# Attention into SwiGLU on one core: the transposes of half-batch 4 moved from TensorE to DMA

## The chip, the cores and the metric

The kernel runs on one core of a Trainium2 chip. The metric is the device time of one execution in microseconds (us), taken as the median of several runs. A profile is one further execution with its own time.

A core has five engines, each with its own queue of instructions that it works through in order: TensorE (PE, with PEld for its weight loads), VectorE (DVE), ScalarE (ACT), GpSimd (POOL) and SyncE (SP). In this kernel SyncE does no arithmetic: it issues transfers. Results of matmuls lie in eight PSUM banks, which other engines read and so free again.

## The reference

For 8 batches of 8 heads, 576 positions and 64 dimensions, causal attention with a decay term taken from `s`, and then a SwiGLU block over all 4608 tokens with `DM` = 512 and `DF` = 1536:

```python
scores = scale * np.matmul(q, k.transpose(0, 1, 3, 2))
cum = np.cumsum(np.maximum(s, 0.0), axis=-1)
bias = -(cum[:, :, :, None] - cum[:, :, None, :])
scores = np.where(causal, -1000000000.0, scores + np.minimum(bias, 0.0))
attn = np.exp(scores - np.max(scores, axis=-1, keepdims=True))
attn = attn / (np.sum(attn, axis=-1, keepdims=True) + 1e-09)
x = np.matmul(attn, v)          # to (B*S, H*D)
g = x @ w_gate
out = (g * (1.0 / (1.0 + np.exp(-g))) * (x @ w_val)) @ w_out
```

## The kernel before

Heads are numbered 0 to 63 (`bh`, or `kk` in the loop). Four heads make a half-batch (`hb`, 0 to 15), eight a batch. For each half-batch, k and q arrive as float32 (`load_qk`, L140, tiles `rawk` and `rawq` with three buffers), are cast to bfloat16 (`cast_one`, L244 on ScalarE or L246 on the others, tiles `ck` and `cq`) and have to be transposed into the score operand `KQ[hb % 2]`, of which there are two. Its other rows, `aug`, carry the decay term and come by DMA from `HL` (L183).

There are two ways to transpose. Half-batches below `NPE` = 5 go over TensorE: `prep_one` transposes 128x128 blocks with the identity (L287), five or four to a bank, and `pe_out` copies each bank out in two halves (L314 on ScalarE, L316 on VectorE). Half-batches from 5 on go over a scratch in DRAM: `scratch` writes `ck` and `cq` to `ks` and `qs` (L260), `transposes` reads them back with two transposing DMAs into `pk` and `pq` (L270), all issued by SyncE, and `split` copies the halves into `KQ` on VectorE (L274, four copies per half-batch). `pk` and `pq` have one buffer each.

For each head, `score_piece` makes four chunks of scores (L359), ScalarE takes the exponential into `pt` (L369), GpSimd masks the diagonal chunks (L374, L379), `av_piece` multiplies by V (L396), and VectorE divides by the row sum (`rc` L412, `ot` L413). V arrives in five chunks per batch (`load_v`, L157, one buffer `rawv`) and is cast into `VT` (L166, L168). The result, transposed into `XT`, feeds the second block: in tiles of 512 tokens, gate and value products (L629), a tanh on ScalarE (`th`, L650), two VectorE instructions that free the gate bank and the value bank (`pp` L652, `ht` L663), and the output product (L686, or L735 in a form with seven products).

The order of all instructions is written by hand (`manual_schedule`). After a prologue with heads 0 to 7, the loop at L1003 walks through the items of the nine token tiles and, between them, pumps `attn_items`, which walks through heads 8 to 63. Loads, casts, scratch writes, transposes and copies of coming half-batches are hung onto certain heads (`h`, `step`) and chunks (`ci`) in `side`. Copies of `split` go onto a list, `later`, from which the loop takes one at some items, and all at the first head of a half-batch. SyncE's queue keeps the program's order: an issue that waits for a cast or for another transfer holds every issue behind it.

The part that matters lies around heads 12 to 20 (`h` = 3 and 4). In the kernel before, SyncE there has, in this order: five loads of V 1, loads of k and q 4, of k and q 5 (all in the prologue), five loads of V 2 (issued at head 12), k and q 6, the scratch writes and transposes of half-batch 5 (head 16), k and q 7, two chunks of V 3, the scratch writes of half-batch 6, three chunks of V 3, the transposes of half-batch 6. Here V n is batch n's V.

Of the kernel before, what the change touches and what calls it, by code (L numbers as in the profile page):

```python
# [19 lines left out]
def kernel(  # L20
# [14 lines left out]
    B, H, S, D = q.shape  # L35
# [6 lines left out]
    NHB = BH // HB  # L42
    NR = HB // 2
# [33 lines left out]
        tc.tile_pool(name="dram", bufs=1, space=bass.MemoryType.DRAM)  # L77
    )

    NPE = 5  # L80
    XB = 2
    KS = {i: dram.tile([NR * S, 128], BF16, name=f"ks{i}") for i in range(NPE, NHB)}
    XS = {
        i: dram.tile([NCH * 128, 128], BF16, name=f"xs{i}") for i in range(XB * H // 2, BH // 2)
    }
    QS = {i: dram.tile([NR * S, 128], BF16, name=f"qs{i}") for i in range(NPE, NHB)}

# [16 lines left out]
    first = first_sbuf.enter_context(tc.tile_pool(name="first", bufs=1))  # L104
# [5 lines left out]
    with tc.manual_schedule():  # L110
# [36 lines left out]
        def load_qk(hb):  # L147
            load_one(hb, "k")
            load_one(hb, "q")

        def load_v(b, cs, eng=nc.sync):
            if 0 in cs:
                loaded["v", b] = raw.tile([128, NCH, H, D], FP32, tag="rawv", bufs=1, name="rawv")
            t = loaded["v", b]
            for c in cs:
                n = 128 if c < 4 else TAIL
                eng.dma_start(  # L157
                    t[0:n, c, :, :],
                    v[b, :, c * 128 : c * 128 + n, :].rearrange("h p d -> p h d"),
                )  # L160
# [97 lines left out]
        def scratch(hb):  # L258
            for name, SC in (("k", KS), ("q", QS)):
                nc.sync.dma_start(  # L260
                    SC[hb].rearrange("(x j) c -> x (j c)", j=J),
                    cts[name, hb].rearrange("x j r d -> x (j r d)"),
                )
# [3 lines left out]
        def transposes(hb):  # L267
            for name, SC in (("k", KS), ("q", QS)):
                prs[name, hb] = cp.tile([128, NR * S], BF16, tag="p" + name, bufs=1, name="p" + name)
                nc.sync.dma_start_transpose(prs[name, hb], SC[hb])  # L270
# [184 lines left out]
        later = []  # L455

        def do_later(n):
            while n > 0 and later:
                f, *args = later.pop(0)
                f(*args)  # L460
                n -= 1
# [5 lines left out]
        def side(h, step, ci):  # L467
            bh = HB * h + step
            for c in V1_AT.get((bh, ci), ()):
                cast_v(1, c, nc.gpsimd)  # L470
            if bh == H + 4 and ci == 3:
                load_v(2, range(5))
            if h == 4 and (step, ci) in ((0, 1), (2, 1)):
                load_qk(6 + step // 2)
            if h >= 5 and h + 3 < NHB and (step, ci) == (0, 1):
                load_qk(h + 3)
            hb = h + 1
            if NPE <= hb < NHB:
                late = hb == NPE
                if late and (step, ci) == (0, 1):  # L480
                    scratch(hb)
                if late and (step, ci) == (0, 3):
                    transposes(hb)
                if (step, ci) == (0, 1):
                    aug(hb, GP4)
                first = 1 if hb < NPE + 3 else 0
                if step in (first, first + 1) and ci == (3 if late else 1):
                    for r in range(NR):
                        later.append((split, hb, "kq"[step - first], r))
            hb = h + 2  # L490
            if hb == NPE and step == 3 and ci % 2 == 1:
                cast_one(hb, "kq"[ci // 2], nc.gpsimd)
            if NPE < hb < NHB:
                six = hb == NPE + 1
                if (step, ci) == ((2, 0) if six else (0, 2)):
                    cast_one(hb, "k", nc.scalar)
                if (step, ci) == ((2, 2) if six else (1, 2)):
                    cast_one(hb, "q", nc.scalar)
                if (step, ci) == ((3, 0) if six else (2, 0)):
                    scratch(hb)  # L500
                if (step, ci) == (3, 3 if six else 0):
                    do_later(NR * 2)
                    transposes(hb)
            if ci != 1:
                return
            bn = h // 2 + 1
            if 3 <= bn < B:
                if h % 2 == 0:
                    if step == 2:
                        load_v(bn, (0, 1))  # L510
                    if step == 3:
                        load_v(bn, (2, 3, 4))
# [4 lines left out]
        def side_v(h, step, ci):  # L517
            bn = h // 2 + 1
            if h == 4 and (step, ci) in V2_AT:
                cast_v(2, V2_AT[step, ci], nc.gpsimd)  # L520
            if 3 <= bn < B and h % 2 == 1 and (step, ci) in V_AT:
                cast_v(bn, V_AT[step, ci], nc.scalar)
# [3 lines left out]
        def prep_one(hb, i, eng=None):  # L526
# [7 lines left out]

        PREP_AT = {
            2: {(1, 2): 0, (2, 0): 2, (2, 2): 1, (3, 0): 3},
            3: {(1, 3): 0, (2, 1): 1, (2, 3): 2, (3, 1): 3},
        }

        AV_AT = {  # L540
# [6 lines left out]
        def attn_items():  # L547
            for kk in range(H, BH + 2):
                h, step = divmod(kk, HB)
                if kk < BH:  # L550
                    if step == 0:
                        do_later(NR * 2)
                    if step == 1 and 3 < h + 1 < NPE:
                        cast_one(h + 1, "k", nc.gpsimd)
                        cast_one(h + 1, "q", nc.gpsimd)
                    if step == 2 and 3 < h + 1 < NPE:
                        aug(h + 1, GP4)
                    for ci in range(4):
                        score_piece(kk, ci)
                        side(h, step, ci)  # L560
                        side_v(h, step, ci)
                        yield kk + 0.1 + ci / 8
                        if (step, ci) in PREP_AT.get(h, ()):
                            prep_one(
                                h + 1, PREP_AT[h][step, ci],
                                (nc.scalar, nc.vector)[ci // 2] if h == 2 else None,
                            )
                            yield kk + 0.1 + ci / 8
                for x in X_AT.get(kk, (kk - 2,)):
                    if x % 2 == 1 and H <= x < BH:  # L570
                        if x < XB * H:
                            x_pe(x // 2)
                            yield kk + 0.5
                        else:
                            x_in(x // 2)
                for p in AV_AT.get(kk, (kk - 1,)):
                    if H <= p < BH:
                        av_piece(p, (0, 1, 2))
                        yield kk + 0.6
                        av_piece(p, (3,))  # L580
                        yield kk + 0.7
                        av_piece(p, (4,))
                        av_out(p)
                        if p >= XB * H and p % 2 == 1:
                            x_out(p // 2)
                        yield kk + 0.8
# [369 lines left out]
        aug(3, SP4)  # L956
        load_v(1, range(5))
        load_qk(4)
        load_qk(5)
        x_pe(0, nc.vector)  # L960
        values(4, 5)
        x_pe(1, nc.scalar)
# [40 lines left out]
        for tt in range(NTT):  # L1003
            lo = H * (tt + 1) + LAGS[tt]
            hi = min(H * (tt + 2) + LAGS[tt + 1], BH + 2)
            span = 36 if tt < FIRST7 else 34.5
            if hi == BH + 2:
                span = 30
            n0 = 5 if tt == 0 else 0
            n = 0  # L1010
            todo = {FIRST7 - 1: W_SUMS, FIRST7: W_DIFFS}.get(tt, [])
            if tt == FIRST7:
                for _ in range(3):
                    weight_op(*todo.pop(0))
            for i, cost in enumerate(ffn_items(tt)):
                n += cost
                if todo and (i >= 24 if tt < FIRST7 else i % 2 == 1):
                    weight_op(*todo.pop(0))
                if tt == 0 and n > 30:
                    pass  # L1020
                elif i >= 2 * NFT or i % (2 if tt == 1 else 4) == 1:
                    do_later(1)
                if seconds:
                    seconds.pop(0)()
                for f in hook.pop(n, ()):
                    f()
                done = min(1.0, max(0, n - n0) / (span - n0))
                if tt == 0:
                    done = (
                        0.57 * max(0, n - n0) / (24 - n0) if n < 24  # L1030
                        else min(1.0, 0.57 + 0.43 * (n - 24) / (span - 24))
                    )
                pump(lo + (hi - lo) * done)
# [31 lines left out]
```

## Time and profile before

| | |
|---|---|
| median of 3 runs | 377.03 us (375.74 to 377.14) |
| the profiled execution's own time | 375.79 us |
| its span (first to last instruction) | 374.0 us |
| granted TensorE clock | 0.999 |
| TensorE busy | 360.7 us, 96% |
| VectorE, ScalarE, GpSimd busy | 289.6, 240.4, 212.3 us |
| hardware DMA queue (SyncE's) | 41.46 MB, 45.2% of 16 engines' span |
| software DMA queue (GpSimd's) | 22.21 MB, 22.6% |

The page cuts the span into 40 slices of 9.35 us, with a digit per slice for the busy tenths of each engine. The chain of waits goes back from the last instruction to whatever released it, step by step. The order in time lists the instructions of one engine with start, duration, line, output and input; in brackets stands how long the engine stood idle before and what ended that. "SPq" rows are SyncE's issues, not the transfers: their duration is the time for which SyncE was held by the issue. The trace also has a record of each semaphore that a transfer fills when it has landed; these are the landing records.

### The profile page before, as it was taken

Reading aid. Unit: us, or ns where it says so; the run is one execution under the profiler, and the core shown is the slowest. Engines: PE = TensorE matmul, PEld = TensorE weight load, DVE = VectorE, ACT = ScalarE, POOL = GpSimd, SP = SyncE. Lnnn points to the kernel's source line nnn. Section 1 sums busy time; section 2 is a strip of 40 time slices with the busy share of each in tenths; the row PEclk is TensorE's granted clock in tenths of the full one; section 3 lists DMA queues with packets and bytes.
Section 4 is the critical chain, followed back from the end, with each engine's and each line's share of the span. In section 5 each row is a group of like instructions: output and inputs, shape, how many; then the busy total and the mean of one; then the engine's idle time right before and its main releaser. Section 6 shows DMA issues by size and latency. Waiting matters only on the chain.

```text
span 374.0 us, 8759 instructions
## 1 busy us (share of the span) xinstructions
PE 360.7 (96%) x3259; PEld 230.6 (62%) x3300; DVE 289.6 (77%) x578; ACT 240.4 (64%) x471; POOL 212.3 (57%) x325
## 2 busy tenths in 40 slices
PE   7799899999999999999999999999999999999995
PEld 6584456655555556855685559655865585476464
DVE  8968776468995899588967997699858867975984
ACT  8777677698876877588757875686566523323321
POOL 8883555856455647494649464955675516315320
PEclk9999999999999999999999999999999999999999
DMA  7899999799877997896779675984132103002003
GB/s 239 193 258 253 219 257 267 237 303 247 245 186 220 254 262 196 178 281 205 211 167 266 178 182 174 255 206 98 40 119 62 35 19 128 2 0 95 20 0 114
DMA packets 97146, 64.23 MB, mean 172 GB/s; under 512 B 77232, under 2 KB 82736, under 8 KB 97104
## 3 DMA queue, kind: packets, MB, share of 16 engines
q1 hardware_dynamic: 84976, 41.46, 45.2%
q0 software_dynamic: 12128, 22.21, 22.6%
q8 instruction: 26, 0.43, 0.5%
q14 instruction: 16, 0.13, 0.1%
HBM read 37.90 MB, written 19.86 MB: 154 GB/s over the span
## 4 chain that ended last, share of the span: by engine, by line
PE 85%; DMA 6%; POOL 5%; ACT 1%; issue 1%; DVE 1%; DVEq 0%; POOLq 0%; ACTq 0%
PE bank L629 45%; PE bank L735 17%; PE bank L359 10%; PE bank L396 7%; PE bank L686 5%; DMA rawk<-in_k_dram 4%; DMA rawv<-in_v_dram 2%; POOL rawv L157 1%; POOL vt L168 1%; POOL wv L332 1%; ACT pt L369 1%; PE bank L287 0%; POOL rawq L140 0%; ACT kq L314 0%; POOL kq L211 0%
## 5 line engine op out<-in xcount | busy, mean ns | idle before, releaser
L369 ACT ACTIVATE pt<-bank 128x512 bf16<-128x512 f32 (+1 forms) x256 | 120.4, 510 | 31.0 <-PE bank L359 18.2
L629 PE MATMUL bank<-XT,wg 128*128 128x512 bf16 x418 | 110.3, 379 | 1.2 <-DVE pp L652 0.3
L629 PE MATMUL bank<-XT,wv 128*128 128x512 bf16 x412 | 109.3, 379 | 1.1
L650 ACT ACTIVATE th<-bank 128x512 bf16<-128x512 f32 x108 | 64.7, 599 | 55.9 <-PE bank L629 53.6
L652 DVE SCALAR_TENSOR_TENSOR pp<-th,bank 128x512 bf16<-128x512 bf16 x108 | 73.6, 682 | 19.2 <-ACT th L650 18.7
L663 DVE SCALAR_TENSOR_TENSOR ht<-pp,bank 128x512 bf16<-128x512 bf16 x108 | 74.1, 686 | 10.6 <-PE bank L629 0.4
L359 PE MATMUL bank<-kq 128*128 128x128 bf16 (+4 forms) x576 | 75.6, 240 | 1.5 <-DMA kq<-HL 1.0
L672 POOL TENSOR_TENSOR ht<-ht 128x512 bf16<-128x512 bf16 x35 | 40.4, 1154 | 52.2 <-DVE su L670 52.1
L359 PEld LDWEIGHTS <-kq 128*128 128x128 bf16 x576 | 45.8, 98 | 31.5 <-issue 1.9
L629 PEld LDWEIGHTS <-wv 128*128 128x128 bf16 x432 | 38.4, 98 | 36.5 <-issue 0.6
L629 PEld LDWEIGHTS <-wg 128*128 128x128 bf16 x432 | 38.3, 98 | 34.2 <-issue 0.7
L396 PEld LDWEIGHTS <-pt 128*128 128x128 bf16 x960 | 41.9, 98 | 17.2
L374 POOL TENSOR_SCALAR_AFFINE_SELECT pt<-pt 128x512 bf16<-128x512 bf16 x56 | 36.8, 658 | 27.3 <-ACT pt L369 22.7
L396 PE MATMUL bank<-vt,pt 128*128 128x65 bf16 x960 | 47.0, 194 | 0.4 <-POOL vt L168 0.3
L430 POOL DMA_DIRECT2D xs<-ot x24 | 21.7, 905 | 30.0 <-DVE ot L413 27.6
L735 PEld LDWEIGHTS <-ht 128*128 128x128 bf16 x336 | 31.2, 98 | 4.3
L413 DVE TENSOR_TENSOR ot<-bank,rc 128x320 bf16<-128x320 f32 x64 | 31.5, 492 | 2.2
L183 POOL DMA_DIRECT2D kq<-HL x48 | 28.9, 604 | 0.0
L735 PEld LDWEIGHTS <-su 128*128 128x128 bf16 x252 | 23.5, 98 | 3.3
L686 PE MATMUL bank<-wo,ht 128*128 128x512 bf16 x90 | 24.8, 379 | 0.3
L800 POOL TENSOR_TENSOR ysb<-ysb 128x512 f32<-128x512 f32 x12 | 15.2, 1270 | 15.3 <-DVE ysb L794 15.3
L379 POOL TENSOR_SCALAR_AFFINE_SELECT pt<-pt 128x64 bf16<-128x64 bf16 x56 | 14.8, 264 | 15.8 <-ACT pt L369 15.7
(93 smaller groups left out, 384.6 us busy)
## 6 DMA issues: line engine op xcount, KB each, us to landing
out_dram<-ysb POOLq DMA_DIRECT2D x32, 256.0 KB, 4.5
rawv<-in_v_dram SPq DMA_DIRECT2D x28, 256.0 KB
rawk<-in_k_dram SPq DMA_DIRECT2D x12, 576.0 KB
rawq<-in_q_dram SPq DMA_DIRECT2D x12, 576.0 KB
xs<-ot POOLq DMA_DIRECT2D x24, 160.0 KB, 3.5
ks<-ck SPq DMA_DIRECT2D x11, 288.0 KB
qs<-cq SPq DMA_DIRECT2D x11, 288.0 KB
rawk<-in_k_dram POOLq DMA_DIRECT2D x3, 576.0 KB, 7.3
```

The source lines that it names most:

```text
L359: nc.tensor.matmul(sc[:, o : o + w], T[:, 1, e * S + 128 * tj : e * S + 128 * (tj + 1)], T[:, 0, e * S + lo : e * S + hi], start=not maske ...
L369: nc.scalar.activation(pt[:, c0 : c0 + n], sc, AF.Exp, scale=0.125)
L374: nc.gpsimd.affine_select(pt[:, 1088:1600], pt[:, 1088:1600], pattern=[[0, 4], [1, 128]], compare_op=ALU.is_ge, fill=zreg, base=0, channel ...
L396: nc.tensor.matmul(av[:, bi * (D + 1) : (bi + 1) * (D + 1)], pt[:, c0 : c0 + 128], VT[b % 2][:, tj, h, :], start=(tj == 0), stop=(tj == bi),)
L413: nc.vector.tensor_mul(ot[:, :, e * D : (e + 1) * D], av3[:, :, 0:D], rc[:, :, None].to_broadcast([128, NCH, D]),)
L629: nc.tensor.matmul(view(bs, TT), w[:, c, f0 : f0 + 128], xt[:, c, :], start=(c == 0), stop=(c == 3),)
L650: nc.scalar.activation(th, pg, AF.Tanh, scale=0.5)
L652: nc.vector.scalar_tensor_tensor(pp, in0=th, scalar=1.0, in1=pg, op0=ALU.add, op1=ALU.mult)
L663: nc.vector.scalar_tensor_tensor(hp[:, 2 * k2 : 2 * k2 + 2, :].rearrange("p a n -> p (a n)"), in0=pp, scalar=0.5, in1=pv, op0=ALU.mult, op ...
L672: (nc.vector if ft == NFT - 1 else nc.gpsimd).tensor_sub(hp[:, 1:3, :], hp[:, 1:4:2, :], hp[:, 0:3:2, :])
L686: nc.tensor.matmul(view(pys[ts_], DM), hps[ft // 2][:, 2 * (ft % 2) + half, c0 : c0 + 128], WO[j][:, ft % WKO, :], start=(ft == 0), stop=( ...
L735: nc.tensor.matmul(ps, lhs(p), rhs(p), start=(first and p == 0), stop=(last and p == NP - 1), skip_group_check=True,)
```

## The change

`NPE` becomes 4, so half-batch 4 no longer goes over TensorE, and gets scratch tensors `ks4` and `qs4`. A new constant `NSC` = 5 keeps the places of all later half-batches as they were. For half-batch 4 the scratch writes are issued at head 13, chunk 3, and its transposes at head 14, chunk 0; the loads of k and q 5 move from the prologue to directly behind these, and the five loads of V 2 from head 12 to behind those. Its four copies are put on `later` at heads 14 and 15, and the loop now takes them in the stretch of the first token tile where it took nothing. The casts of half-batch 4 stay on GpSimd at head 13.

By engine: TensorE loses 18 transposes, ScalarE four copies out of PSUM; on VectorE four copies out of PSUM make way for four out of `pk` and `pq` at nearly the same places, and the rest of its order is unchanged; GpSimd's order is unchanged; SyncE gets two scratch writes and two transposes between the loads of q 4 and k 5, and the rest of its order is unchanged.

```diff
-    NPE = 5
+    NPE = 4
+    NSC = 5
@@ side(h, step, ci)
-            if bh == H + 4 and ci == 3:
-                load_v(2, range(5))
+            if h == 3:
+                if (step, ci) == (1, 3):
+                    scratch(4)
+                if (step, ci) == (2, 0):
+                    transposes(4)
+                    load_qk(5)
+                    load_v(2, range(5))
+                if (step, ci) in ((2, 3), (3, 1)):
+                    for r in range(NR):
+                        later.append((split, 4, "kq"[step - 2], r))
@@ (further down in side: every NPE becomes NSC)
-            if NPE <= hb < NHB:
-                late = hb == NPE
+            if NSC <= hb < NHB:
+                late = hb == NSC
...
@@
         PREP_AT = {
             2: {(1, 2): 0, (2, 0): 2, (2, 2): 1, (3, 0): 3},
-            3: {(1, 3): 0, (2, 1): 1, (2, 3): 2, (3, 1): 3},
         }
@@ attn_items
-                    if step == 1 and 3 < h + 1 < NPE:
+                    if step == 1 and h == 3:
                         cast_one(h + 1, "k", nc.gpsimd)
                         cast_one(h + 1, "q", nc.gpsimd)
-                    if step == 2 and 3 < h + 1 < NPE:
+                    if step == 2 and h == 3:
                         aug(h + 1, GP4)
@@ prologue
         load_qk(4)
-        load_qk(5)
@@ main loop
                 if tt == 0 and n > 30:
-                    pass
+                    if later and later[0][1] == 4:
+                        do_later(1)
```

## The prediction

> **What bounds the kernel now.** I read the page first (span, engines, the 40 slices), then the table of busy time by stages, then the chain of waits around the change (50 to 90 us), then the order in time of SyncE's issues, POOL and DVE there. Half-batch n holds heads 4n to 4n+3; "k 4", "V 2" and so on name a transfer's data.
>
> ```profile
> span 374.0 us, 8759 instructions
> PE 360.7 (96%) x3259; PEld 230.6 (62%) x3300; DVE 289.6 (77%) x578; ACT 240.4 (64%) x471; POOL 212.3 (57%) x325
> PEclk9999999999999999999999999999999999999999
> DMA  7899999799877997896779675984132103002003
> ```
>
> TensorE is busy 96% of the span and its clock is never lowered, so what comes off PE's queue is time won, and an interval in which PE must stand is time lost. DMA is near nine tenths through the first quarter: a transfer put into that stretch delays the transfers behind it. By stages:
>
> ```profile
> 60.00:70.00 10.00, 9.89 (x130) 6.79 (x130) 6.91 (x15) 5.90 (x12) 5.00 (x8) 1.00 0.95 255
> 70.00:80.00 10.00, 9.89 (x86) 5.71 (x87) 2.85 (x7) 8.97 (x18) 9.51 (x18) 1.00 0.79 208
> 80.00:90.00 10.00, 9.77 (x101) 5.75 (x101) 8.72 (x18) 7.62 (x15) 5.12 (x10) 1.00 1.25 321
> ```
>
> (Columns: stretch, length, then busy us of PE, PEld, DVE, ACT, POOL, clock, DMA share, GB/s.) The removed work lies in the first of these, where PE is full and DVE and ACT are not. In the last, DVE is close to full: it could not catch up there. SyncE's issues:
>
> ```profile
> 54.18 9.56 SPq L157 DMA_DIRECT2D rawv<-in_v_dram  x5
> 63.85 0.55 SPq L140 DMA_DIRECT2D rawk<-in_k_dram  x1
> 68.21 0.36 SPq L260 DMA_DIRECT2D ks<-ck  x1
> 69.49 0.35 SPq L260 DMA_DIRECT2D qs<-cq  x1
> 71.14 1.74 SPq L270 DMA_TRANSPOSE pk<-ks  x1
> 72.98 1.29 SPq L270 DMA_TRANSPOSE pq<-qs  x1
> ```
>
> Five V issues take 9.56 us although one alone takes 0.37 to 0.6: SyncE is held by its own full queue. The trace's landing records (when a transfer's semaphore is full) show the queue served in order: q 4 at 56.5, q 5 59.8, V 2 61.0 to 66.3, k 6 67.9, q 6 69.4, ks 5 70.2, qs 5 71.4, pk 5 75.3, pq 5 77.3, q 7 81.9, pk 6 93.1. On the other side stand those who use them:
>
> ```profile
> 56.88 1.15 POOL L246 CAST cq<-rawq 128x1152 bf16<-128x1152 f32 x1 [1.45 <-DMA rawq<-in_q_dram]
> 79.58 0.45 DVE L274 COPY kq<-pk 64x1152 bf16<-64x1152 bf16 x1
> 79.95 0.67 DVE L652 SCALAR_TENSOR_TENSOR pp<-th,bank 128x512 bf16<-128x512 bf16 x1
> 84.39 0.95 DVE L274 COPY kq<-pq 64x1152 bf16<-64x1152 bf16 x1
> ```
>
> and, in the chain of waits, PE's first score of half-batch 5 (head 20):
>
> ```profile
> 85.37 0.12 issue
> 85.49 0.38 PE bank L359 x4
> ```
>
> The copy out of pk 5 starts 4.3 us after pk 5 has landed, and head 20's score starts 0.15 us after the first copy out of pq 5 (84.39 + 0.95 = 85.34): that score has no slack against DVE.
>
> **The change, part by part** (times on the clock of this profile).
>
> *Removed from PE, ACT, DVE.* 18 transposes (L287); between other matmuls the chain of waits books five at 0.28 us and four at 0.22, together 1.0 us, from a PE that is full: −1.0. Bounds: 0, if a later wait takes it, and −2.2, with the 1.2 us for which DVE stood waiting for these L287 added. ACT loses four copies (1.5 + 1.5 us), DVE four (1.6 + 1.4), and gains four copies out of pk and pq at 0.45 = 1.8 us: nothing, since both have 3 us free in 10 there. Four banks fewer are taken: nothing.
>
> *Half-batch 4 by DMA.* The casts stay where they are on POOL: ck 4 ends 54.30 + 1.13 = 55.4, cq 4, which waits for q 4, ends 58.0. SyncE issues ks 4 at 55.5 and qs 4 at 58.1 (0.36). pk 4 is issued at 58.5 (ks landed 2.0 us after its issue for half-batch 5, so by 57.5), and pq 4 when qs has landed, about 60.1, until 61.4. A transpose landed 4.2 and 4.3 us after its issue: 62.7 and 64.4. The four copies stand on DVE where the four L316 stood (61.9 to 68.3): the first comes about 62.8 and the third, out of pq 4, about 65.8; head 16's score comes at 67.9 (68.90 less 1.0). Cost 0, with some 0 to 3.5 us of cover; 2 us at most if the transposes take half as long again.
>
> *What stands behind them on SyncE.* k 5 and q 5 are now issued at 61.4 instead of 45.6, V 2 after that, then k 6 and q 6, ks 5, qs 5 and pk 5. q 7 landed 4.6 us after pq 5, so q 5 lands at 64.4 + 4.6 = 69.0, 9.2 us later than now. V 2 needs 6.5 us (59.8 to 66.3): 75.5. k 6 77.1, q 6 78.6, ks 5 79.4. pk 5 is issued then and lands 4.2 later: 83.6, against 75.3 now, +8.3; pq 5 about 85.5. Bounds: without the stores to out that shared the DMA while q 7 came, q 5 lands 3.1 us after pq 4 (as q 6 after V 2), and T4 might take 1 us less: +5.5; with these stores (73 to 80 us) now beside V 2 and half-batch 6: +10.5. I keep 8.3.
>
> *Waiters in between.* POOL's cq 5 cast (68.32) waits for q 5 till 69.0; behind it on POOL stand a mask (L374, 70.03) and four aug issues, all with about 2 us before use: 0, at most 1. ACT's cast of k 6 (76.51, 75.5 after the gain) waits till 77.1 with th (L650) and exps behind it: up to 1.6, which eats the 1.0 won but falls ahead of the next, longer wait, so it isn't added. V 2's casts on POOL (74.38 to 79.1) come after their landing (70.2 to 75.5): 0.
>
> *DVE at pk 5, the step that decides.* DVE reaches the first copy of half-batch 5 at about 79.6 (78.6 if the whole gain got there) and stands till 83.6. Behind it wait pp (79.95), which frees a gate bank, ht, rc and ot. PE takes that gate bank again at 81.70, so it runs on for 2.1 us and then stands. From 83.6 DVE works through its 4.8 us of queue up to the copy out of pq 5, which ends 0.45 to 0.95 later: 83.6 + 4.8 + 0.6 = 89.0. Head 20's score starts at 89.1 in place of 85.49: **+3.6** net, the 1.0 already inside. Bounds by pk 5's: +0.8 (80.8) to +5.8 (85.8).
>
> *Half-batch 6.* It has less slack: pk 6 landed at 93.1 and its copy started at 93.77, that is 97.4 in the shifted time; behind pq 5 the queue is full up to there (q 7, V 3, ks, qs), so pk 6 keeps about 8 of its 8.3 us: 101. DVE stands 3.5 us, PE is covered for about 2.1 to 2.5: **+1.0** (0 to +3.5). Head 24's score (103.01 + 3.6 = 106.6) then finds its copies done at 101 + 5.3 = 106.3. At half-batch 7 the copy (109.14) came 3.4 us after pk 7 (105.7), and SyncE stood 3 us for ks 7, so with 4.6 us of compute shift the queue has caught up: 0.
>
> Sum: +4.6 against the profiled execution's 375.8: 380.4. The median of the runs is 1.2 above that execution, which makes 381.6; I take 381.0, between.
>
> *A rule weighed.* Rows: nine blocks by DMA landed in 4.2 us, about 0.47 us each, and PE did one in 0.056 us of its queue. The Trainium skill (VectorE: DVE Perf Modes, "The three transpose paths" and the rules below it) says to use TensorE for 128×128 where PSUM will do and gives 1309 ns for the DMA way. An estimate by that figure, 18 × 1.3 = 23.6 us in a row, would land pq 4 near 82, put head 16 some 14 us late and the time near 390. The row is a third of it, so it decides; the rule's direction stands against this change.
>
> **Rivals.**
> - *The queue catches up* (the other side). The hardware queue fills 45% of the engines over the span, and V 2 no longer has k 5, q 5 and the weights' tail ahead of it. If pk 5 lands by 79.6, head 20 is not late; at 78.6 or before, the whole 1.0 stays: 376.0 on the runs' scale, at best 374.8 with the 1.2 above. That needs a shift of pk 5 below 3.3 us where the two transposes alone hold the queue from 58.5 to 64.4. Against it: the order of landings.
> - *The delay stays*: half-batches 6 and 7 wait too, PE's cover being used up by a DVE that is 87 to 90% busy. PE then ends with all of pk's 8.3: 377.0 + 8.3 = 385.3.
> - *Half-batch 4 itself is late*: pq 4 after 67.9 rather than 64.4 (q 4 later, or transposes at half speed) moves head 16 and everything behind; 2 us more: 383.5.
>
> **How the numbers follow.** Half a per cent is 1.9 us, about what a measurement of this kernel tells from no change. Forecast (+2.5 to +6.5) 0.56; delay stays 0.13; half-batch 4 late 0.09; queue catches up or lands near 80 us (−2.2 to +1.9) 0.22, of which over 1.9 us faster 0.05. So faster 0.05, same 0.17, slower 0.78. The range, 376.0 to 386.0, takes in the rival at its working value and the whole 8.3; the forecast's own is 379 to 384.
>
> **What will show it.** Right: SyncE's k 5 issue near 61 to 62 and pk 5 near 79; a DVE idle of 3 to 5 us before L274, released by DMA pk; head 20's L359 about 3.6 us later; L287 18 fewer. Wrong: no DVE idle before L274 between 75 and 100 us (then the queue was not full), or the first idle already at head 16.

## The result and the profile after

The changed kernel takes 382.07 us (median of 5 runs, 380.71 to 384.54) against 377.03 before. The ratio on record, taken from the runs of the two, is 1.0159 with a 95% interval of 1.0122 to 1.0196; the two medians alone give 1.0134. The profiled execution took 384.54 us, the slowest of the five, with a span of 382.5 us. From its page:

```profile
span 382.5 us, 8725 instructions
PE 365.7 (96%) x3241; PEld 232.2 (61%) x3282; DVE 288.6 (75%) x578; ACT 237.5 (62%) x467; POOL 212.6 (56%) x325
...
PEclk9999899996999999999999999999999999999999
```

TensorE has 18 matmuls fewer and yet 5.0 us more of busy time. The clock row says most of why: two slices (the fifth and the tenth) are below full speed (half the clock from 41.6 to 45.0 us and from 86.0 to 92.8). In the busy table by stages the loss is in one stretch (columns as before: stretch, length, busy us of PE, PEld, DVE, ACT, POOL, clock, DMA share, GB/s):

```profile
70.00:80.00 10.00, 9.89 (x86) 5.74 (x87) 2.68 (x8) 7.96 (x16) 9.69 (x19) 1.00 1.18 279
80.00:90.00 10.00, 6.60 (x57) 3.66 (x57) 5.39 (x12) 4.72 (x9) 1.67 (x4) 0.80 1.04 298
90.00:100.00 10.00, 9.95 (x77) 5.34 (x77) 7.04 (x14) 6.56 (x14) 5.09 (x9) 0.86 0.96 227
```

Between 80 and 90 us PE is busy for 6.60 us, where it was 9.77, and at a clock of 0.80. SyncE's issues in order of time:

```profile
58.23 0.36 SPq L261 DMA_DIRECT2D ks<-ck  x1
...
60.36 1.31 SPq L271 DMA_TRANSPOSE pk<-ks  x1
...
63.16 0.53 SPq L141 DMA_DIRECT2D rawk<-in_k_dram  x1
...
64.26 8.41 SPq L158 DMA_DIRECT2D rawv<-in_v_dram  x5
72.78 0.56 SPq L141 DMA_DIRECT2D rawk<-in_k_dram  x1
...
73.94 0.42 SPq L261 DMA_DIRECT2D ks<-ck  x1
...
81.61 1.25 SPq L271 DMA_TRANSPOSE pk<-ks  x1
```

V 2 is first issued at 64.26 (54.18 before), and the transposes of half-batch 5 at 81.61 (71.14 before). The landing records here: ks 4 60.3, pk 4 63.8, pq 4 67.4, k 5 69.1, q 5 70.7, V 2 72.0 to 76.0, k 6 77.6, q 6 80.2, ks 5 81.6, pk 5 85.7, pq 5 86.8, pk 6 100.5. In the kernel before they are k 5 59.8, q 5 61.6, V 2 62.4 to 66.8, k 6 68.7, q 6 70.3, ks 5 71.1, pk 5 75.6, pq 5 77.5, q 7 82.9 and pk 6 93.3; the prediction had some of them up to 1.8 us too early. VectorE and TensorE there, in order of time (the bracket is the idle time before, and what ended it):

```profile
65.67 0.44 DVE L275 COPY kq<-pk 64x1152 bf16<-64x1152 bf16 x1
...
85.71 0.45 DVE L275 COPY kq<-pk 64x1152 bf16<-64x1152 bf16 x1 [4.27 <-DMA pk<-ks]
86.09 0.67 DVE L660 SCALAR_TENSOR_TENSOR pp<-th,bank 128x512 bf16<-128x512 bf16 x1
...
86.81 0.59 PE L637 MATMUL bank<-XT,wv 128*128 128x512 bf16 x1 [3.18 <-DVE pp L660]
...
89.33 1.91 PE L637 MATMUL bank<-XT,wg 128*128 128x512 bf16 x4
...
93.24 0.39 PE L360 MATMUL bank<-kq 128*128 128x128 bf16 x4
```

VectorE stands 4.27 us for pk 5, `pp` behind it is late, and PE, which waits for the gate bank that `pp` frees, stands 3.18 us. Then four products that took 1.03 us elsewhere take 1.91, at half the clock. The last line is head 20's first score, at 85.49 before. The chain of waits goes the same way (start, length, what), with SyncE's queue as its first link:

```profile
73.94 7.62 DMA ks<-ck
81.61 4.08 DMA pk<-ks
85.71 0.45 DVE kq L275
86.16 0.61 DVE pp L660
```

ks 5 was issued only 1.27 us after the last V 2 was off SyncE's hands, but lands 7.62 us later, behind V 2, k 6 and q 6.

**Where the 8.5 us of the two profiled spans come from.** The same VectorE instruction in both traces, after less before: +2.6 at 44 us already, ahead of the first place where the two queues of SyncE differ (45.6 us); +2.8 at 58.5; +1.7 at 63.6; +6.1 at the first copy out of pk 5; +7.8 at 100; +8.9 at the copy out of pk 8 (a wait of 1.51 us); +8.55 at the end. So 2.6 to 2.8 us arose ahead of anything that the change moves: in the prologue PE stood 2.12 us for the cast of k 3 (1.16 before) and ran at half clock from 41.6 to 45.0. The rest, 5.8 us, comes behind it and is near what all runs say (5.0 by the medians, 6.0 by the ratio). That all of it, and nothing but it, is the change's is an assumption: the repeat below has no late prologue and ends 9.1 us behind.

### The profile page after: what moved, and what is told of

Read it like the earlier page. It is cut to its first block, busy times and chain, and to the rows that moved or that the text cites. A ratio compares the mean times of both kernels' runs of the same rounds, so it can differ in the third digit from the quotient of the medians.

```text
span 382.5 us, 8725 instructions
## 1 busy us (share of the span) xinstructions
PE 365.7 (96%) x3241; PEld 232.2 (61%) x3282; DVE 288.6 (75%) x578; ACT 237.5 (62%) x467; POOL 212.6 (56%) x325
## 3 DMA queue, kind: packets, MB, share of 16 engines
q0 software_dynamic: 12128, 22.21, 22.8%
## 4 chain that ended last, share of the span: by engine, by line
PE 82%; DMA 6%; DVE 4%; POOL 3%; ACT 2%; issue 1%; DVEq 0%; SPq 0%; POOLq 0%; ACTq 0%
PE bank L637 43%; PE bank L743 17%; PE bank L360 10%; PE bank L397 7%; PE bank L694 5%; DMA pk<-ks 3%; DMA ks<-ck 2%; ACT pt L370 2%; DVE pp L660 1%; DVE ht L671 1%; DVE kq L317 1%; DMA kq<-HL 1%; POOL vt L169 1%; PE bank L354 1%; PE bank L446 1%
## 5 line engine op out<-in xcount | busy, mean ns | idle before, releaser
L637 PE MATMUL bank<-XT,wv 128*128 128x512 bf16 x411 | 111.5, 385 | 4.5 <-DVE pp L660 3.2
L637 PE MATMUL bank<-XT,wg 128*128 128x512 bf16 x419 | 111.9, 383 | 1.3 <-DVE pp L660 0.3
```

The costliest lines, as they stand in the source:

```text
L637: nc.tensor.matmul(view(bs, TT), w[:, c, f0 : f0 + 128], xt[:, c, :], start=(c == 0), stop=(c == 3),)
```

## The experiments

Times are medians with the ratio to the kernel before on the same chip, and its 95% interval. "After" is the changed kernel; diffs are against it unless another is named.

**The changed kernel once more** (no edit), to see what repeats.

> The changed kernel as it is, profiled a second time. Theory (the wait for the transposed k of half-batch 5 costs the time): VectorE stands 3.5 to 5 us before its first copy of half-batch 5, released by the transposing DMA, PE stands about 3 us for the gate bank behind it, and the granted clock halves for 3 to 7 us right after. The 2.8 us that the first profile of the changed kernel was late by before any changed issue, and the 1.2 us lost at half-batch 8, are of that execution: here the first is within 1 us of the kernel before, and the second may be gone. Rival (the change itself slows the prologue): again 2 us or more late by head 12.

Measured: 384.74 us (one run; before 375.91).

```profile
65.33 0.45 DVE L275 COPY kq<-pk 64x1152 bf16<-64x1152 bf16 x1 [2.63 <-DMA pk<-ks]
...
86.95 0.45 DVE L275 COPY kq<-pk 64x1152 bf16<-64x1152 bf16 x1 [5.13 <-DMA pk<-ks]
...
88.05 0.58 PE L637 MATMUL bank<-XT,wv 128*128 128x512 bf16 x1 [4.89 <-DVE pp L660]
```

The prologue was on time here (−0.3 us against the first profile of before, at 44 us). VectorE waited 2.63 us for pk 4, 5.13 us for pk 5 (PE 4.89 us behind it, then half clock from 87.5 to 90.9) and 0.89 us for pk 6. The wait at pk 5 and its effect on PE repeat; the +2.6 of the prologue doesn't. The wait at pk 4, absent in the first profile, is there with the prologue on time. Nor is the total smaller for it: the shift against before is +0.2 us at 69 us, +2.2 at 78, +7.4 at the first copy out of pk 5 (which landed at 86.9), +7.6 at 100 and +9.1 at the end. Single executions of one kernel can end some us apart.

**Unused transfers on the kernel before.** Half-batch 4 keeps its TensorE transposes; its scratch writes and DMA transposes are issued as well, and nothing reads them, with k, q 5 and V 2 behind them as in the change.

```diff
(against the kernel before)
...
-            if bh == H + 4 and ci == 3:
-                load_v(2, range(5))
+            if h == 3:
+                if (step, ci) == (1, 3):
+                    scratch(4)
+                if (step, ci) == (2, 0):
+                    transposes(4)
+                    load_qk(5)
+                    load_v(2, range(5))
...
         load_qk(4)
-        load_qk(5)
```

> The kernel before with its TensorE transposes of half-batch 4 kept and used, and beside them the two scratch writes and two transposing DMAs of half-batch 4, whose result nothing reads, in the changed kernel's places, with k, q 5 and V 2 behind them. Theory (what stands behind these transfers on SyncE's queue is late): VectorE waits at the copies of half-batch 5 as in the changed kernel; 382 to 384 us, that is the changed kernel's time plus up to the 1.0 us of PE work that is back. Rival (half-batch 4's own copies out of pk and pq, or its scores, are the cost): nothing of half-batch 4 waits for these transfers, so 376 to 378.

Measured: 382.04 us, 1.0174 (1.0147 to 1.0201), which can't be told from the changed kernel's ratio.

```profile
84.71 0.45 DVE L274 COPY kq<-pk 64x1152 bf16<-64x1152 bf16 x1 [4.22 <-DMA pk<-ks]
...
85.81 0.58 PE L634 MATMUL bank<-XT,wv 128*128 128x512 bf16 x1 [4.03 <-DVE pp L657]
```

The wait for pk 5 is there in full although half-batch 4 is transposed where it always was. So the transfers added to SyncE's queue, with the loads moved behind them, are enough for the whole loss. What half-batch 4's own use of the transposed data costs, and what TensorE is spared (1.0 us), can't be told from the medians, since both intervals are 2 us wide or more.

**k and q 5 back in the prologue.** V 2 stays behind the transposes.

```diff
                     transposes(4)
-                    load_qk(5)
                     load_v(2, range(5))
...
         load_qk(4)
+        load_qk(5)
```

> The changed kernel with the loads of k, q 5 back in the prologue; V 2 stays behind the transposes of half-batch 4. Theory (order in SyncE's queue): the queue in front of the transposes of half-batch 5 is shorter by what the loads of half-batch 5 wait now for the scratch round trip; k 5's transpose lands 2 to 4 us sooner than in the changed kernel, VectorE's wait there falls from 4.3 to 0.5 to 2.5 us, which PE's free banks cover mostly; 376.5 to 379. Rival (the 1.2 MB more that the DMA engines move, wherever it stands): the transposes of half-batch 5 land as late as in the changed kernel, 381 to 383.

Measured: 380.28 us, 1.011 (1.0082 to 1.0138), between the two expectations. The interval overlaps that of the change's own (1.0122 to 1.0196) by a little, so some gain is likely but small.

```profile
66.80 0.55 DVE L275 COPY kq<-pk 64x1152 bf16<-64x1152 bf16 x1 [3.08 <-DMA pk<-ks]
...
84.16 0.45 DVE L275 COPY kq<-pk 64x1152 bf16<-64x1152 bf16 x1 [2.52 <-DMA pk<-ks]
```

ks 4, now behind k and q 5, lands at 63.1 (60.3 in the change) and half-batch 4 waits; V 2 is issued at 65.89, pk 5 lands at 84.1 (85.7 in the change's first profile, whose prologue was 2.8 us late; 86.9 in the repeat). The wait at half-batch 5 gets shorter and one at half-batch 4 comes in its place.

**V 2 in front as well.** Both groups of loads are back at their old places, and the transposes of half-batch 4 stand behind them.

```diff
             if h == 3:
+                if (step, ci) == (0, 3):
+                    load_v(2, range(5))
                 if (step, ci) == (1, 3):
                     scratch(4)
                 if (step, ci) == (2, 0):
                     transposes(4)
-                    load_qk(5)
-                    load_v(2, range(5))
...
         load_qk(4)
+        load_qk(5)
```

> The changed kernel with the loads of k, q 5 back in the prologue and the load of V 2 back in the third chunk of head 12, so that the two DMA transposes of half-batch 4 stand behind V 2 in SyncE's queue. Theory (SyncE's queue has no free place: whichever transfer stands in front, the next consumer is late): V 2 is first issued at about 54 us as before, the transposes of half-batch 4 land at 70 to 73 us, VectorE waits 3 to 7 us at the first copy of half-batch 4 and head 16 is 3 to 5 us late, while the first copy of half-batch 5 waits at most 1.5 us; 378 to 381 us. Rival (only the late loads cost; with them in front everything is restored): the wait at half-batch 4 is under 1.5 us and the time 375 to 377.5 us.

Measured: 383.52 us, 1.0199 (1.0149 to 1.0248): the theory's place, but above its 381.

```profile
71.17 0.45 DVE L275 COPY kq<-pk 64x1152 bf16<-64x1152 bf16 x1 [8.37 <-DMA pk<-ks]
...
72.31 0.58 PE L360 MATMUL bank<-kq 128*128 128x320 bf16 x2 [6.70 <-DVE ot L414]
```

V 2 is first issued at 54.01, as in the kernel before, pk 4 lands at 71.1, VectorE stands 8.37 us (3 to 7 expected) and PE 6.70. The shift against before is 7.8 us at 77 us and 7.7 at the end, and half-batch 5 has no wait at all. The rival, that only the late loads cost, is out: with all loads in front, half-batch 4 pays instead.

**The copies of half-batch 5 moved back on VectorE**, from heads 17 and 18 to the end of head 19, so that `pp` and others go ahead of them.

```diff
-                if step in (first, first + 1) and ci == (3 if late else 1):
+                if late and (step, ci) in ((3, 1), (3, 2)):
+                    for r in range(NR):
+                        later.append((split, hb, "kq"[r], 0) if ci == 1 else (split, hb, "kq"[r], 1))
+                if not late and step in (first, first + 1) and ci == 1:
```

> The changed kernel, all transfers in the same order, but VectorE's four copies of half-batch 5 moved down its order from heads 17 and 18 to the end of head 19, behind eight other instructions, as k, q, k, q. Theory (VectorE stands in line at a copy that nobody needs yet, and holds the gate bank): the transpose lands as late as before, about 7 us after the kernel before, but VectorE's wait falls below 1.5 us and PE's to under 1.5 us, no halved clock follows; 376.5 to 379. Rival (the data are too late for head 20's scores, wherever the copies stand): PE waits at head 20 for 3 us or more instead, 380 to 383.

Measured: 381.48 us, 1.0152 (1.0126 to 1.0178). At half-batch 5 VectorE doesn't wait any more and PE only 0.91 us, but:

```profile
98.14 0.45 DVE L275 COPY kq<-pk 64x1152 bf16<-64x1152 bf16 x1 [4.25 <-DMA pk<-ks]
...
99.25 0.19 PE L360 MATMUL bank<-kq 128*128 128x64 bf16 x1 [2.00 <-DVE pp L663]
```

The wait reappears one half-batch later, nearly as long, and half-batch 8 waits 1.28 us. The waits at half-batch 5 go as the theory said, but the time doesn't: the delay in SyncE's queue is still there when pk 6 is due, which lands at 98.1 (93.3 before).

**All copies from half-batch 5 on moved back** to the end of the half-batch before, on the changed kernel and on the kernel before.

```diff
-                if step in (first, first + 1) and ci == (3 if late else 1):
+                if (step, ci) == ((3, 1) if late else (2, 3)):
                     for r in range(NR):
-                        later.append((split, hb, "kq"[step - first], r))
+                        for name in "kq":
+                            later.append((split, hb, name, r))
```

On the changed kernel:

> The changed kernel with VectorE's four copies of every half-batch from 5 on moved to the end of the half-batch ahead of it (where its next transpose is issued), all transfers in the same order. Theory (the queue is late by a fixed amount, 7 us at half-batch 5, 4.8 at 6, and it costs only where a copy stands ahead of its need): no wait of VectorE over 1.5 us for a transpose between 75 and 140 us; 375.5 to 378. Rival (the queue has no slack anywhere, the delay reappears at half-batch 7 or 8): 379.5 to 382.

On the kernel before:

> The kernel before with the same move of VectorE's copies of half-batches 5 and on to the end of the half-batch ahead. Theory (the copies had 0 to 4 us of slack there already, and moving them removes no wait): 375 to 377, the same as before. If it is faster by over 1 us, part of what the later copies win in the changed kernel is not the change's own cost; if it is slower by over 1 us, head 20's scores and those like it wait for the moved copies.

Measured: 384.77 us, 1.0243 (1.0211 to 1.0275), and 378.09 us, 1.0069 (1.0054 to 1.0083). The edit itself costs 0.7%, so with it the change still costs 1.7%. From half-batch 5 on VectorE waits less than 1 us for pk or pq (1.83 us at pk 4 remain), but now PE stands for a transposing DMA of the second block:

```profile
123.33 0.59 PE L638 MATMUL bank<-XT,wg 128*128 128x512 bf16 x1 [2.28 <-DMA XT<-xs]
```

Against before, VectorE is 1.1 us late at 99 us and 5.0 at 135, while the kernel before with the same edit is not late at either. Where no copy waits, the next user of SyncE's queue does.

**V 2 issued by GpSimd**, whose transfers go through the other DMA queue, at heads 13 to 15.

```diff
             if h == 3:
+                for c in {(1, 3): (0, 1), (2, 0): (2,), (2, 2): (3,), (3, 0): (4,)}.get((step, ci), ()):
+                    load_v(2, (c,), nc.gpsimd)
...
                     load_qk(5)
-                    load_v(2, range(5))
```

> The changed kernel with the five loads of V 2 issued by GpSimd on its own queue, at heads 13 to 15, in place of SyncE behind the transposes of half-batch 4; k, q 5 stay behind these. Theory by order (SyncE's queue is served in its order, and V 2's 6.5 us in it are the bulk of the delay): k 5's transpose lands by 78 to 80 us, VectorE waits for it under 1.5 us; 376 to 378.5. Rival by amount (the DMA engines are full, so V 2 beside the others slows these as much as V 2 ahead of them): it lands at 82 to 86, wait and time as in the changed kernel, 380 to 383.

Measured: 381.91 us, 1.0161 (1.0142 to 1.018).

```profile
68.03 0.45 DVE L275 COPY kq<-pk 64x1152 bf16<-64x1152 bf16 x1 [5.61 <-DMA pk<-ks]
...
69.17 0.38 PE L360 MATMUL bank<-kq 128*128 128x320 bf16 x2 [3.94 <-DVE ot L414]
```

pk 4, issued at 59.53, lands at 68.0: 8.5 us, where it took 3.4 in the change. pk 5 lands at 84.2 (85.7 in the change, with its prologue 2.8 us late), but nothing waits for it, since the compute is late already. Landing and time are the rival's; the wait stands at half-batch 4, where neither had it. Between 60 and 70 us the row by stages has the DMA share at 1.18 and 217 GB/s (0.96 and 222 in the change): the DMA engines are busier there and move no more, so freeing SyncE of V 2 doesn't free them.

**Half the dose**: only k of half-batch 4 goes by DMA, q over TensorE as before.

```diff
...
-                    scratch(4)
+                    scratch(4, "k")
...
-                    transposes(4)
+                    transposes(4, "k")
...
-                if (step, ci) in ((2, 3), (3, 1)):
+                if (step, ci) == (2, 3):
...
             2: {(1, 2): 0, (2, 0): 2, (2, 2): 1, (3, 0): 3},
+            3: {(2, 1): 1, (3, 1): 3},
```

> The changed kernel with half the change: only k of half-batch 4 goes over the DRAM scratch, q is transposed on TensorE as before; k, q 5 and V 2 stay behind the one transpose. Theory by amount (the transfers added ahead of half-batch 5 make it late by what they take of the DMA, 7 us for two): half the delay, k 5's transpose lands 3 to 4.5 us later than before, at 78.5 to 80, VectorE waits under 1.5 us for it; 375.5 to 378.5. Rival by round trip (the loads wait for a write to DRAM and a transpose behind it, whose latency is nearly the same for one as for two): it lands after 81.5, 379.5 to 382.

Measured: 380.65 us, 1.0127 (1.0087 to 1.0167).

```profile
84.46 0.45 DVE L275 COPY kq<-pk 64x1152 bf16<-64x1152 bf16 x1 [3.92 <-DMA pk<-ks]
```

With half of the bytes the wait is 3.92 us instead of 4.27, V 2 is first issued at 61.67 and pk 5 lands at 84.4, where the rival by round trip had it. So the loss doesn't go by the number of bytes transposed. Before V 2 comes SyncE's stand for the cast of k 4 and for the landing of ks 4 (issued 56.83, landed 59.1), and that is the same for one transpose as for two.

**The four stores of the first token tile's output held back to head 23**, on the changed kernel and on the kernel before, to take their bytes out of the stretch.

```diff
+        held = []
...
+            if h == 5 and (step, ci) == (3, 1):
+                while held:
+                    held.pop(0)()
...
-                stores.append(
+                (held if tt == 0 else stores).append(
```

On the changed kernel:

> The changed kernel with the four stores of the first token tile (1 MB, on GpSimd's queue between heads 16 and 18) held back until head 23. Theory by amount: k 5's transpose lands 2 to 3.5 us sooner than in the changed kernel although nothing on SyncE's queue has moved, VectorE's wait of 4 to 5 us falls to 1 to 2.5; 377.5 to 380.5. Rival by order alone (only what stands ahead on SyncE's own queue counts): it lands where it did, 381 to 383.

On the kernel before:

> The kernel before with the same four stores held back until head 23, as the measure for that move alone. Both theories: nothing there waits for what these stores delay, 375 to 377; if the four issues in a row (2.4 us of GpSimd) hold masks that are needed, up to 378.5.

Measured: 382.28 us, 1.0167 (1.0131 to 1.0203), and 376.83 us, 1.0032 (1.0 to 1.0065). pk 5 lands at 85.4 as without the edit, and VectorE's wait for it (2.62 us, in an execution with the prologue 2.8 us late) is there. The stores are not what makes pk 5 late.

**Fifty dummy matmuls** (128x128, their result read by nothing) in the stretch where PE stands, ahead of the value products that wait, to keep the clock up.

```diff
+        def fill(n):
+            b = sorted(bank, key=lambda x: released[x])[1]
+            for _ in range(n):
+                nc.tensor.matmul(view(b, 128), ident, ident, start=True, stop=True)
...
+                if tt == 1 and ft == 2:
+                    fill(50)
                 vbs = products("v", ft, xt)
```

> The changed kernel with 50 matmuls of 128 by 128 on the identity, whose result nothing reads, on PE just ahead of the value product at which PE stands for 3 to 5 us (into a bank that stands free there). Theory (the clock is halved because PE stood): the halved stretch of 3.4 us after that wait goes or moves, PE's wait there shrinks to under 1.5 us, and the time falls by about 1 to 2 us, to 380 to 381. Rival (the halving comes by itself): it stays, 381.5 to 383.

Measured: 381.05 us, 1.0139 (1.0119 to 1.0158).

```profile
86.13 0.45 DVE L275 COPY kq<-pk 64x1152 bf16<-64x1152 bf16 x1 [4.22 <-DMA pk<-ks]
```

The profile shows full clock from 4.6 to 380 us, while VectorE's wait for pk 5 is still 4.22 us; PE stands 1.34 us. That the matmuls hold the clock is likely, not shown: the run with the stores held back kept full clock behind a stand of 2.75 us without them. The time can't be told from the changed kernel's (1.0122 to 1.0196), so what the halved clock costs in the medians stays open. The traces say more: from the first copy out of pk 5 to head 20's first score it takes 5.9 us before, 5.9 here, 6.0 in the repeat and 6.3 with the unused transfers (half clock for 3.4 us in both) and 7.5 in the change's first profile (6.8 us). The shorter stretch of half clock cost 0.1 to 0.4 us there, the longer about 1.6.

No version beat the kernel before.

## Why the prediction was right, point by point

The forecast of 381.0 us (379 to 384) was 1.1 us below the measured 382.07, and the chain of waits is the predicted one. Part of the closeness of the number is luck, since errors in the parts offset each other and single executions differ by more than the forecast's error. Times of the first profile are set back below by its prologue's 2.8 us.

- *What stands behind on SyncE*: right in the first profile. k 5's issue at 60.4 (predicted 61.4), half-batch 5's transposes issued at 78.8 (79.4), pk 5 landed at 82.9 (83.6), pq 5 at 84.0 (85.5). Without any setting back, pk 5 landed at 83.4 to 84.7 in the two runs with moved copies and the one with unused transfers, but at 86.1 with the dummy matmuls and 86.9 in the repeat, above the prediction's bound of 85.8. The parts were less right than their sum: the landings were misread (q 7 came 5.4 us after pq 5, not 4.6; V 2 took 5.1 us, not 6.5), and in the change q 5 came 3.4 us after pq 4 (4.6 predicted) and V 2 took 5.3 (6.5), but q 6 took 2.5 (1.5) and ks 5 1.4 (0.8). From V 2's first issue to pk 5's landing it is 21.4 us before and in the change and 21.2 with the unused transfers: there the delay came in ahead of V 2. It is no constant, though: 22.8 with half the dose, 18.3 with k and q 5 in front. The prediction's reason for the 9.56 us of V's issues, a full queue, is a reading that no record here shows.
- *DVE at pk 5*: right. The wait was predicted at 83.6 less 78.6 to 79.6, so 4 to 5 us, and was 4.27 and 5.13; behind it PE stands, through `pp` and the gate bank, as written.
- *Waiters in between*: right in kind. ScalarE's cast of k 6 did not wait in the first profile, waited 1.83 us in the repeat (up to 1.6 predicted) and 0.6 to 1.3 in three variants, and in the repeat and with the dummy matmuls the longer wait at pk 5 came behind it, as written. V 2's casts weren't quite free: PE stood 0.92 us for one in the repeat.
- *Head 20 +3.6*: the place is right, the size short. Head 20's score came 5.0 us late in the first profile (set back) and 7.4 in the repeat. The sum had 5.5 us from pk 5's landing to that score. VectorE's queue alone takes 5.9 to 6.0 from the copy, in the kernel before as in the repeat and with the dummy matmuls. In the first profile it was 7.5, with the clock halved for 6.8 us. So the excess there is the clock's, as far as one trace tells, and in the repeat it is pk 5's later landing.
- *Half-batch 6, +1.0*: this term of the sum failed. There was no wait there in the first profile and 0.89 us in the repeat. Its step kept 8 of the 8.3 us for pk 6; pk 6 landed 7.2 us later than before, 4.4 set back. So of the 7.3 us by which pk 5 was late, set back, SyncE's queue had made up 2.9 by pk 6, while the compute was 5.0 late by then and not the 3.6 of the sum. In the repeat pk 6 did keep 8.8 us, but VectorE came to its copy 7.5 us late and waited little. The loss at pk 5 had covered the one that was booked here. The run with the moved copies, where the compute came earlier, shows that half-batch 6 is the next to wait (4.25 us).
- *Half-batches 7 and 8, 0*: 7 right; at 8 there was a wait of 1.51 us that the prediction didn't have. That copy had waited 0.34 us in the kernel before already, so it had no slack. In the repeat it is missing, and a wait of 2.10 us stands at 254 us instead. So these two last errors make up for each other by luck, −1.0 and +1.1 in the first profile.
- *Half-batch 4 by DMA, 0, at most 2*: 0 in the first profile, but 1.0 to 3.1 us of VectorE's time in the repeat and four of the variants, in none of which the prologue was 2 us late. pk 4 landed at 63.6 to 66.8 in these, against 62.7 predicted. It mostly hides in the later wait at pk 5, and with the loads in front it becomes the larger one (3.08 and 8.37 us). As a rival it was priced at 2 us and given too little room: the prediction named a first idle at head 16 as a sign of being wrong, and the repeat has it, though the loss there is gone again by 69 us (+0.2).
- *Removed work, −1.0*: there (the shift goes from +2.8 to +1.7 around 62 us), and then it falls ahead of the wait at pk 5, which ends with the transfer and not with the compute. That it is lost is read from this order; the medians of the kernel with unused transfers, which lacks the 1.0, are too wide to tell 1 us.
- *The queue catches up* (the rival on the other side): out. It needed a shift of pk 5 below 3.3 us; it was 7.3 set back, and 11.4 in the repeat.

Not settled: how the delay divides between SyncE's order and the DMA engines' load. Half the dose and the held stores speak for the order and the stand for ks 4; V 2 on GpSimd's queue says that the order alone isn't all, since a transpose then takes 8.5 us. No run moved the loads of k, q 5 and V 2 without adding a transfer, so the price of the later loads alone isn't known either; with all loads at their old places the added transfers still cost as much (1.0199).

## What to carry to other kernels

A transfer that waits for a round trip (cast, write to scratch, read back) in a queue that issues in order delays every issue behind it, so price it by the next consumer behind it in the queue, not by the work it replaces: here a saving of 1.0 us on a full TensorE came with some 5 us of lateness one half-batch later. Before you reorder such a queue to mend that, look for a free place in it; here each order tried (loads behind, half in front, all in front, V elsewhere) changed who waited more than how long. A kernel with unused transfers on the old path is a cheap way to tell the cost of the place from the cost of the route.

## What the runs showed of the hardware that was not expected

- *The clock falls after short stands of PE, but not after every one.* Stands of 2.00, 2.10, 2.12, 2.28, 2.51, 2.83, 3.18, 3.94, 4.03, 4.89 and 6.70 us were each followed or overlapped by half clock for 3.4 us (6.8 us with 3.18 and with 6.70); stands of up to 1.67 us were not, nor were one of 2.15 us (in the prologue of the run with the dummy matmuls) and one of 2.75 (with the stores held back). With the 2.00 us stand (97.2 to 99.3 us) the half clock ran from 101.5 to 104.9, when PE was busy again. The Trainium skill (TensorE: Matmul & The Clock Gate, "Part 1: The HAM clock gate") says that the clock is halved after at least one idle window of about 3.4 us, and that the window runs freely. The length of 3.4 us agrees with these rows; that a stand must be that long does not, since 2.0 us was enough here.
- *The same transpose, of k 4, took 3.1 to 8.5 us from issue to landing* (1152 rows of 128), by what else was under way: 3.1 with half the dose, 3.4 in the change, 8.5 with V 2 on the other queue.
- *An issue of V held SyncE for 0.37 us or for 4.0*: in the row x5 of the change the five issues took 0.46, 1.57, 4.02, 1.01 and 1.16 us, and in the change a later one alone 0.37. SyncE loses this time in issuing, apart from any wait that the program has; what holds it isn't recorded.
